# Attention and a gated MLP in one kernel: the last group takes x's seven combinations from DRAM, h's sums move to VectorE, partial sums are added by transfers

## The chip, the cores and the metric

One Trainium2 chip, one core. The metric is device microseconds of one execution, the median of the runs. All matrices are float32; the q, k, v, weight inputs arrive as float64 words and are converted on the chip.

## The reference, cut to what matters

```python
# q, k, v: (8, 8, 576, 64); block-causal softmax attention per head, then
x = attn_out.transpose(0, 2, 1, 3).reshape(4608, 512)
gate = 1.0 / (1.0 + np.exp(-(x @ w_gate)))      # w_gate, w_val: (512, 1536)
val = x @ w_val
return (gate * val @ w_out).astype(np.float32)  # w_out: (1536, 512)
```

## The kernel before, in words

The 1536 hidden columns are worked in three groups of 512. **The first group** runs beside the attention, batch by batch, with ordinary products; its output (a partial sum of the result, 4608 x 512) goes to the DRAM tensor `part_d`, and the attention output goes, transposed, to `xT_d`. **The second group** (the first loop over `k` near the end, six blocks of 768 tokens) and **the last group** (the second loop, again six blocks) use a seven-product scheme: the 2 x 2 blocks of a matrix product are formed from seven products of sums of blocks instead of eight products. Here they are called the second stage and the last stage.

A float32 product is made of three matmuls on "high" and "low" parts (a rounded copy, and the difference to it), so one of the seven products is 6 matmuls of 128x384 (`product`). Both loops need the seven combinations of x as high and low parts, 14 tiles called `XO` (names `XH`, `XL` in the trace). Per block they are made in this way: `x_load` brings x's four quarters from `xT_d` into `XB`, `x_sums` makes three sums on POOL, and `x_split` (second stage, lines 1196 to 1210) or `x_split_slots` (last stage, lines 1177 to 1194) copies the high parts on ACT and subtracts the low parts on VectorE (line 1204 and line 1183). There is one set of `XO`, so a slot is rewritten only when the last of the four units (two column halves, gate and value) has read it.

A block runs four `unit`s (168 matmuls), whose products are evicted by VectorE additions, a tanh on ACT and a multiplication on VectorE (line 1541) that gives h. In the second stage `out_block` then multiplies h by a plain `w_out` (72 matmuls of 128x512); `result` reads the old partial sum from `part_d`, adds on POOL (line 1584) and writes to a second tensor `part2_d`. In the last stage the output product is a seven-product scheme too (`out_terms`, 84 matmuls), so h needs its own sums: `own_halves` and `second_sum` form them on POOL (lines 1433, 1439, 1443, 1447), and split them into five slots `S` (ACT lines 1420, 1424, 1456; VectorE lines 1421, 1425, 1451, 1457). The accumulators `C` of out_terms must be read by an addition at line 1486 before product 3 adds to them (line 1400 is every matmul of `product`). Results are transposed on VectorE (line 1492), added to the partial sum (line 1494; POOL, in the last block VectorE) and stored.

Between the two loops the weights of the last group, converted piece by piece in the second stage (`streamed`, through a staging tile `st` to `wgv_d`), are loaded back: four tiles `w` of 1792 KB as each unit of the last second-stage block ends (line 1679), and two tiles `wo` (line 1689).

The order on each engine is made by a scheduler at build time from data dependencies; `behind(a, b)` adds an order between two instructions of one engine. SP issues nearly all transfers, in order, and waits in that order.

Of the kernel before, what the change touches and what calls it, by code (L numbers as in the profile page):

```python
# [74 lines left out]
def attn_glu_kernel(ctx: ExitStack, tc: tile.TileContext, q, k, v, w_gate, w_val, w_out, out):  # L75
# [162 lines left out]
    with ExitStack() as s2:  # L238
# [819 lines left out]
        part2_d = dram.tile([NTOK, DM], F32, name="part2_d")  # L1058
# [63 lines left out]
        def fetch_o(g, d, j, held=False):  # L1122
            raw, T = cv_tiles()
            rawv = raw.rearrange("p (kh mh c n) w -> p kh mh c (n w)", kh=2, mh=2, c=4)
            r = (F1 + 4 * g + 2 * j) * P
            cols = w_out.rearrange("r (mh c e n) -> r mh e c n", mh=2, c=4, e=2)[:, :, d]
# [49 lines left out]

        def x_split_slots(XBs):

            def split(a, b, src):
                for j, XB in enumerate(XBs):  # L1180
                    x = XB[:, src:src + b - a]
                    nc.scalar.copy(out=XO[j][0][:, a:b], in_=x)
                    low = nc.vector.tensor_sub(out=XO[j][1][:, a:b], in0=x, in1=XO[j][0][:, a:b].bitcast(F32))  # L1183
                    if a in (3, 6) or (a == 1 and j):
                        for fh in range(2):
                            behind(low.ins, last2[f"B22{fh}"])

            split(0, 1, 0)
            for XB in XBs:
                nc.gpsimd.tensor_sub(out=XB[:, 0], in0=XB[:, 2], in1=XB[:, 5])  # L1190
            split(4, 6, 4)
            split(1, 3, 1)
            split(3, 4, 3)
            split(6, 7, 0)
# [196 lines left out]
        XO = [[x2.tile([P, 7, N2], F32R, name=f"X{e}{j}") for e in "HL"] for j in range(KC)]  # L1391
# [22 lines left out]
        def own_halves(q, i, h):  # L1414

            SL, B11, B12, B22, sums = terms
            fh, second = divmod(i, 2)

            def split(slot, x, low):
                nc.scalar.copy(out=slot[:, 0], in_=x)  # L1420
                low.tensor_sub(out=slot[:, 1], in0=x, in1=slot[:, 0].bitcast(F32))

            def part(slot, x, low):
                nc.scalar.copy(out=slot[:, 0, fh], in_=x)
                ins = low.tensor_sub(out=slot[:, 1, fh], in0=x, in1=slot[:, 0, fh].bitcast(F32))  # L1425
                if slot is SL[2]:
                    mark2(f"B22{fh}", ins)

            if q == 0:
                if second:  # L1430
                    return
                T1 = sums[fh]
                nc.gpsimd.tensor_sub(out=T1, in0=B12[:, fh], in1=B11[:, fh])
                part(SL[0], h, nc.gpsimd)
                part(SL[1], T1, nc.gpsimd)
                return
            if second:
                part(SL[2], h, nc.vector)
                nc.gpsimd.tensor_sub(out=B12[:, fh], in0=h, in1=B12[:, fh])
                B22.append(h)  # L1440
                if fh:
                    split(SL[4], B12[:, :2], nc.vector)
                    nc.gpsimd.tensor_add(out=B11[:, :2], in0=B11[:, :2], in1=B12[:, :2])
                return
            part(SL[3], h, nc.vector)
            old = B22[fh]
            nc.gpsimd.tensor_sub(out=old, in0=h, in1=B11[:, fh])
            if fh:
                for n, x in enumerate(B22):
                    nc.scalar.copy(out=SL[0][:, 0, n], in_=x)  # L1450
                    nc.vector.tensor_sub(out=SL[0][:, 1, n], in0=x, in1=SL[0][:, 0, n].bitcast(F32))
                B22.clear()

        def second_sum():
            SL, B11, B12, B22, sums = terms
            nc.scalar.copy(out=SL[1][:, 0], in_=B11[:, :2])
            nc.vector.tensor_sub(out=SL[1][:, 1], in0=B11[:, :2], in1=SL[1][:, 0].bitcast(F32))

        def dm_rows(dst, k, m, n):
# [3 lines left out]
                     dst[r:r + N2, 256 * m + 64 * c:256 * m + 64 * c + 64].rearrange("(t p) x -> p t x", p=32))  # L1463
                    for c in range(4)]

        def place(x):
            return x.rearrange("p (t x) -> p t x", x=64)

        def partial(pr, k, m, n):
            for rows_, src in dm_rows(part2_d, k, m, n):  # L1470
                nc.sync.dma_start(out=place(pr)[rows_], in_=src)

        def out_terms(k, Wo, prs, spare, end):
# [4 lines left out]
            p1, c22 = {}, {}  # L1478
            for d in range(2):
                product(1, A[d], Wo[d], True, SL[0])  # L1480
                p1[d] = hp3.tile([P, N2], F32, name="p1o") if d else m2.tile([P, N2], F32, name="p1", bufs=2)
                nc.scalar.copy(out=p1[d], in_=A[d])
            for d in range(2):
                product(5, C[d], Wo[d], True, SL[1])
                c22[d] = spare[d]["22"]()
                nc.vector.tensor_add(out=c22[d], in0=C[d], in1=p1[d])  # L1486
# [3 lines left out]
            def result(m, n, d, c, src=None):  # L1490
                pr = prs[m, n]
                nc.vector.transpose(out=c, in_=c if src is None else src)
                x = place(pr).rearrange("p t (e j) -> p t e j", e=2)[:, :, d]
                (nc.vector if end else nc.gpsimd).tensor_add(out=x, in0=x, in1=c.rearrange("p (t j) -> p t j", j=32))
                if d:
                    for i, (rows_, dst) in enumerate(dm_rows(out, k, m, n)):
                        (nc.scalar if end and i % 2 else nc.sync).dma_start(out=dst, in_=place(pr)[rows_])
# [259 lines left out]
```

## Time and profile before

| | us |
|---|---|
| median of 3 runs (1148.11 to 1155.28) | 1150.37 |
| the profiled execution's own time | 1148.83 |
| its span, first to last instruction | 1147.0 |
| attention with the first group | 0 to about 542 |
| second stage, six blocks | about 542 to 822 |
| last stage, six blocks | about 822 to 1147 |

A block of the second stage lasts 45.7 us, one of the last stage 51.3 to 51.9 us. "PE" is the matmul engine (TensorE), "DVE" VectorE, "ACT" ScalarE, "POOL" GpSimd, "SP" the engine that issues most transfers. A waiting time stands in square brackets in front of the instruction that waited, with what ended it. The granted clock of TensorE has two levels here, 1.00 (2.4 GHz) and 0.50 (1.2 GHz).

### The profile page before, as it was taken

Reading aid. Unit: us, or ns where it says so; the run is one execution under the profiler, and the core shown is the slowest. Engines: PE = TensorE matmul, PEld = TensorE weight load, DVE = VectorE, ACT = ScalarE, POOL = GpSimd, SP = SyncE. Lnnn points to the kernel's source line nnn. Section 1 sums busy time; section 2 is a strip of 40 time slices with the busy share of each in tenths; the row PEclk is TensorE's granted clock in tenths of the full one; section 3 lists DMA queues with packets and bytes.
Section 4 is the critical chain, followed back from the end, with each engine's and each line's share of the span. In section 5 each row is a group of like instructions: output and inputs, shape, how many; then the busy total and the mean of one; then the engine's idle time right before and its main releaser. Section 6 shows DMA issues by size and latency. Waiting matters only on the chain.

```text
span 1147.0 us, 20057 instructions
## 1 busy us (share of the span) xinstructions
PE 1091.6 (95%) x6653; PEld 949.7 (83%) x6653; DVE 959.0 (84%) x1617; ACT 623.4 (54%) x1377; POOL 643.1 (56%) x761
## 2 busy tenths in 40 slices
PE   8999999999999999999999999999888988989895
PEld 6677777877887788788999989999778988989795
DVE  6899989998888898596998897888958778786957
ACT  6888777777777777433535444345332515242321
POOL 3745598989898887101143624625545656647432
PEclk9999999999999999999999999999988989989898
DMA  8797578888888777433324733629964351524152
GB/s 165 169 183 162 152 175 210 178 205 172 208 174 207 169 187 180 150 107 91 113 93 161 267 128 139 224 98 353 318 218 116 73 133 33 138 83 84 28 111 55
DMA packets 341227, 178.02 MB, mean 155 GB/s; under 512 B 287412, under 2 KB 308260, under 8 KB 340356
## 3 DMA queue, kind: packets, MB, share of 16 engines
q1 hardware_dynamic: 321284, 151.42, 50.9%
q0 software_dynamic: 6272, 17.26, 5.9%
q10 hardware_dynamic: 13568, 8.06, 2.6%
q8 instruction: 53, 0.87, 0.3%
q14 instruction: 50, 0.41, 0.1%
HBM read 106.30 MB, written 49.18 MB: 136 GB/s over the span
## 4 chain that ended last, share of the span: by engine, by line
PE 72%; DVE 15%; DMA 4%; issue 2%; POOL 2%; ACT 2%; SPq 1%; DVEq 0%; ACTq 0%; POOLq 0%
PE b L1400 31%; PE bank L368 13%; PE m L180 11%; PE m L191 7%; PE m L1572 5%; DVE XL L1183 3%; PE b L1572 2%; PE bank L180 1%; SPq L302 1%; DVE S L1425 1%; PE m L1400 1%; DVE v L1541 1%; DMA rb<-r_d 1%; DMA wgv_d<-st 1%; DVE XL L1204 1%
## 5 line engine op out<-in xcount | busy, mean ns | idle before, releaser
L1400 PE MATMUL b<-XH,w 128*128 128x384 f32 x1344 | 349.6, 336 | 7.5 <-DVE b L1548 5.4
L1400 PEld LDWEIGHTS b<-XH,w 128*128 128x128 f32 x1344 | 245.0, 189 | 10.8 <-DVE b L1548 5.8
L1400 PE MATMUL b<-XL,w 128*128 128x384 f32 x672 | 225.4, 336 | 0.0
L1400 PEld LDWEIGHTS b<-XL,w 128*128 128x128 f32 x672 | 126.9, 189 | 0.8
L1584 POOL TENSOR_TENSOR pr<-pr,pr 128x512 f32<-128x512 f32 x36 | 57.0, 1591 | 111.1 <-ACT pr L1583 87.6
L1400 PE MATMUL b<-S,wo 128*128 128x384 f32 x360 | 84.6, 389 | 23.1 <-DVE pr L1486 18.4
L1400 PEld LDWEIGHTS b<-S,wo 128*128 128x128 f32 x360 | 74.8, 224 | 30.3 <-DVE pr L1486 20.3
L368 PE MATMUL bank<-G,VS 128*64 128x64 f32 (+3 forms) x1264 | 95.4, 305 | 1.0 <-POOL G L626 0.6
L368 PEld LDWEIGHTS bank<-G,VS 128*64 128x64 f32 x1264 | 64.8, 137 | 33.7 <-issue 7.4
L191 PE MATMUL m<-wo,hH 128*128 128x512 f32 x256 | 84.1, 395 | 0.0
L180 PE MATMUL m<-XH,wg 128*128 128x512 f32 x240 | 81.2, 395 | 1.2 <-ACT t L213 1.2
L180 PE MATMUL m<-XH,wv 128*128 128x512 f32 x240 | 80.8, 394 | 0.0
L497 DVE TENSOR_REDUCE nm<-bank 128x2 f32<-128x1024 f32 (+1 forms) x96 | 76.9, 801 | 2.1 <-ACT XB L509 0.5
L1527 ACT COPY p<-b 128x384 f32<-128x384 f32 x48 | 22.8, 475 | 86.9 <-PE b L1400 84.3
L1537 ACT ACTIVATE g<-g 128x384 f32<-128x384 f32 x72 | 37.6, 525 | 57.4 <-DVE g L1561 28.9
L1572 PE MATMUL m<-wo,hH 128*128 128x512 f32 x192 | 63.5, 397 | 0.0
L191 PEld LDWEIGHTS m<-wo,hH 128*128 128x128 f32 x256 | 47.8, 188 | 10.7 <-ACT ost L986 0.9
L180 PEld LDWEIGHTS m<-XH,wg 128*128 128x128 f32 x240 | 45.1, 188 | 10.7 <-ACT t L213 1.7
L180 PEld LDWEIGHTS m<-XH,wv 128*128 128x128 f32 x240 | 45.0, 188 | 9.6 <-DVE h L217 0.2
L509 ACT ACTIVATE Z<-bank,nm 128x512 f32<-128x512 f32 (+3 forms) x96 | 49.3, 530 | 6.0 <-DVE nm L497 2.5
L191 PE MATMUL m<-wo,hL 128*128 128x512 f32 x128 | 51.3, 401 | 0.0
L509 ACT ACTIVATE XB<-bank,nm 128x512 f32<-128x512 f32 (+3 forms) x96 | 49.3, 530 | 3.5 <-DVE nm L497 1.9
(273 smaller groups left out, 2939.3 us busy)
## 6 DMA issues: line engine op xcount, KB each, us to landing
wgv_d<-st SPq DMA_DIRECT2D x12, 896.0 KB
XB<-xT_d SPq DMA_DIRECT2D x16, 576.0 KB
pr<-part_d SPq DMA_DIRECT2D x36, 256.0 KB
part_d<-pr SPq DMA_DIRECT2D x36, 256.0 KB
rqk<-in_q_dram SPq DMA_DIRECT2D x120, 72.0 KB
rqk<-in_k_dram SPq DMA_DIRECT2D x120, 72.0 KB
w<-wgv_d SPq DMA_DIRECT2D x4, 1792.0 KB
xT_d<-xT SPq DMA_DIRECT2D x24, 288.0 KB
```

Source lines behind the costliest of these rows:

```text
L180: mm = nc.tensor.matmul(ps, lhsT=lh, rhs=rh, start=(i == 0), stop=(i == n - 1))
L191: mm = nc.tensor.matmul(ps, lhsT=lh[:, f, t * P:(t + 1) * P], rhs=rh, start=(f == i == 0), stop=(f == F1 - 1 and i == 2))
L302: ins = queue.dma_start(**kw)
L368: pe_last[:] = [pin("PE", nc.tensor.matmul(*args, **kw)).ins]
L497: mark("DVE", nc.vector.tensor_reduce(out=nm_()[:, c0:c0 + 2], in_=ps[:, :, c:c + n], axis=AX.X, op=ALU.max, negate=True))
L509: mark("ACT", nc.scalar.activation(out=dst, in_=src, func=AF.Exp, bias=nm_()[:, c0 + h:c0 + h + 1], accum_out=sm[:, 5 * h + i:5 * h + i + 1]))
L1183: low = nc.vector.tensor_sub(out=XO[j][1][:, a:b], in0=x, in1=XO[j][0][:, a:b].bitcast(F32))
L1400: mm = nc.tensor.matmul(ps, lhsT=lh, rhs=rh, start=(first and k == 0), stop=(k == n - 1), skip_group_check=not first)
L1527: nc.scalar.copy(out=p1, in_=A)
L1537: mark2("ACT", nc.scalar.activation(out=t, in_=c, func=AF.Tanh, scale=0.5))
L1572: mm = nc.tensor.matmul(po[t], lhsT=lh[:, f, t * P:(t + 1) * P], rhs=wo[:, f, e], start=(half == i == 0), stop=(half == 1 and i == len(tod ...
L1584: nc.gpsimd.tensor_add(out=ost, in0=ost, in1=old)
```

## The change

- The second stage stores the split combinations of each block to a new DRAM tensor `x_d` right after it made them (`x_keep`, seven transfers of 768 KB). The last stage loads them (`x_fetch`, seven transfers in the order in which the products use the slots) instead of loading x and making sums and splits. `x_split_slots` is gone.
- The sums of h are made on VectorE, after the pieces that are due earlier, with `behind` holding them there; POOL keeps only two of them per block (T1 of the first column half).
- The second stage's `result` no longer loads the old partial sum, adds and stores: a transfer issued by POOL adds the block to `part_d` in DRAM. `part2_d` is gone; the last stage loads `part_d` and stores the result in pieces of 128 columns instead of 64.
- The staging tile `st` has two buffers instead of one, and the last conversion of a weight piece comes one place earlier.

```diff
-        part2_d = dram.tile([NTOK, DM], F32, name="part2_d")
+        x_d = dram.tile([NK, P, 7, 2 * KC, N2], F32, name="x_d")
...
+        X_ORDER = (0, 5, 4, 2, 1, 3, 6)
+        def x_keep(k):
+            for i in X_ORDER:
+                nc.sync.dma_start(out=x_d[k, :, i], in_=XOt[:, :, i].bitcast(F32))
+        def x_fetch(k):
+            for i in X_ORDER:
+                nc.sync.dma_start(out=XOt[:, :, i].bitcast(F32), in_=x_d[k, :, i])
...
+        def second_sums(c22):
+            SL, T1, T3 = terms
+            low = halves(SL[1], T1, nc.vector)
+            behind(low.ins, c22)
+            for fh, h in enumerate(seconds):
+                t = nc.vector.tensor_sub(out=T3[:, fh], in0=h, in1=T3[:, fh])
+                behind(t.ins, low.ins)
+            halves(SL[4], T3, nc.vector)
+            seconds.clear()
+        def last_sums(other):
+            SL, T1, T3 = terms
+            for fh, h in enumerate(firsts):
+                t = nc.vector.tensor_sub(out=T1[:, fh], in0=h, in1=T1[:, fh])
+                behind(t.ins, other)
+            halves(SL[0], T1, nc.vector)
+            firsts.clear()
...
-                ost = io.tile([P, DM], F32, name="pr0", bufs=4)
-                old = io.tile([P, DM], F32, name="pr1", bufs=2)
-                nc.sync.dma_start(out=old, in_=part_d[r:r + P, :])
+                ost = io.tile([P, DM], F32, name="pr0", bufs=3)
                 nc.scalar.mul(out=ost, in_=po[t], mul=0.5)
-                nc.gpsimd.tensor_add(out=ost, in0=ost, in1=old)
-                nc.sync.dma_start(out=part2_d[r:r + P, :], in_=ost)
+                nc.gpsimd.dma_start(out=part_d[r:r + P, :], in_=ost, accum_op=ALU.add)
...
-                st = io.tile([P, 2, 7, P], F32R, name="st")
+                st = io.tile([P, 2, 7, P], F32R, name="st", bufs=2)
...
-            if i == 2 or (i == 1 and k) or (i == 0 and k == NK - 1):
+            if (i == 2 and k < NK - 1) or (i == 1 and k) or (i == 0 and k >= NK - 2):
...
-            x_split(XBs, sums)
+            if k < NK - 1:
+                x_split(XBs, sums)
+                x_keep(k + 1)
+            else:
+                x_fetch(0)
...
             if not end:
-                x_split_slots(XBs)
-            for m, n in ((0, 0), (1, 0)):
-                partial(prs[m, n], k, m, n)
+                x_fetch(k + 1)
             run(block)
```

On VectorE, in the last stage's fourth block, from the multiplications that give h to the split of a sum (`XL`: low parts of x; `S`: low parts of h; L1486 the readings of the accumulators), before:

```order
L1541 SCALAR_TENSOR_TENSOR v_10669<-g_10609,v_10669 128x384
L1425 TENSOR_TENSOR S_9087<-t_10646,S_9087 128x384
L1541 SCALAR_TENSOR_TENSOR v_10667<-g_10607,v_10667 128x384
L1425 TENSOR_TENSOR S_9086<-v_10669,S_9086 128x384
L1486 TENSOR_TENSOR g_10745<-b,p_10729 128x384
L1425 TENSOR_TENSOR S_9086<-v_10667,S_9086 128x384
L1183 TENSOR_TENSOR XL_5851<-XB,XH_5850 128x768
L1183 TENSOR_TENSOR XL_5849<-XB,XH_5848 128x384
L1183 TENSOR_TENSOR XL_5851<-XB,XH_5850 128x384
L1486 TENSOR_TENSOR pr_9092<-b,p1o 128x384
L1561 TENSOR_TENSOR v_10668<-b,p_10651 128x384
L1421 TENSOR_TENSOR S_9088<-b_9090,S_9088 128x768
```

The same place in the changed kernel (L1424 and L1441 are h's sums into `XB`, L1473 the readings of the accumulators, L1432 the split of a sum):

```order
L1413 TENSOR_TENSOR S_9001<-t_10412,S_9001 128x384
L1530 SCALAR_TENSOR_TENSOR v_10435<-g_10375,v_10435 128x384
L1544 TENSOR_TENSOR v_10433<-b,v_10433 128x384
L1424 TENSOR_TENSOR XB<-v_10435,XB 128x384
L1530 SCALAR_TENSOR_TENSOR v_10433<-g_10373,v_10433 128x384
L1413 TENSOR_TENSOR S_9000<-v_10435,S_9000 128x384
L1424 TENSOR_TENSOR XB<-v_10433,XB 128x384
L1413 TENSOR_TENSOR S_9000<-v_10433,S_9000 128x384
L1473 TENSOR_TENSOR g_10506<-b,p_10491 128x384
L1473 TENSOR_TENSOR sp_9003<-b,p1o 128x384
L1432 TENSOR_TENSOR S_8999<-XB,S_8999 128x768
L1441 TENSOR_TENSOR XB<-v_10433,XB 128x384
```

The three low parts of x between the two readings of the accumulators are gone; the two readings stand next to each other, with two sums of h ahead of them and four behind.

On SP, where the second stage ends, before (`w` and `wo`: weights of the last stage, `st`: converted pieces, XB<-xT_d: x for the next block):

```order
L1679 DMA w_8689<-wgv_d 128x3584
L1638 DMA wgv_d<-st 128x1792
L1679 DMA w_8779<-wgv_d 128x3584
L1585 DMA part_d<-pr_8581 128x512
L1582 DMA pr_8982<-part_d 128x512
L1091 DMA raw<-in_moe_w_out_dram 128x4x64 x4
L1679 DMA w_8841<-wgv_d 128x3584
L1638 DMA wgv_d<-st 128x1792
L1679 DMA w_8941<-wgv_d 128x3584
L1585 DMA part_d<-pr_8975 128x512
L1582 DMA pr_8988<-part_d 128x512
L1164 DMA XB<-xT_d 128x2x384
```

The same place in the changed kernel (XO<-x_d: the slots of x for the last stage's first block):

```order
L1666 DMA w_8649<-wgv_d 128x3584
L1666 DMA w_8739<-wgv_d 128x3584
L1382 DMA XO<-x_d 128x4x384 x4
L1625 DMA wgv_d<-st 128x1792
L1666 DMA w_8801<-wgv_d 128x3584
L1382 DMA XO<-x_d 128x4x384 x2
L1666 DMA w_8901<-wgv_d 128x3584
L1382 DMA XO<-x_d 128x4x384
L1625 DMA wgv_d<-st 128x1792
L1680 DMA wo_8994<-wgv_d 128x3584
L1680 DMA wo_8995<-wgv_d 128x3584
L1382 DMA XO<-x_d 128x4x384 x7
```

The seven slots stand between the weights of the last stage, in one queue with them, and behind a store of a converted piece.

## Rows read from the trace of the kernel before

**Rows 1.** The page, the span in 40 slices: the clock granted to PE, in tenths

```profile
PEclk9999999999999999999999999999988989989898
```

**Rows 2.** Busy by stretch: stretch, length, PE, PEld, DVE, ACT, POOL, clock, DMA share, GB/s

```profile
695.74:741.48 45.74, 45.74 (x242) 42.75 (x241) 37.77 (x63) 19.78 (x36) 19.54 (x16) 1.00 0.47 153
768.00:815.00 47.00, 44.01 (x220) 40.07 (x219) 42.16 (x72) 20.94 (x36) 20.52 (x17) 0.96 1.01 349
815.00:850.00 35.00, 28.38 (x139) 26.50 (x138) 21.65 (x34) 9.24 (x18) 19.18 (x14) 0.90 0.90 300
887.00:938.30 51.30, 47.06 (x254) 45.92 (x253) 40.03 (x64) 18.80 (x36) 29.74 (x28) 0.93 0.41 94
```

**Rows 3.** PE in order of time, the output product of the last stage's second block

```profile
910.99 2.24 PE L1400 MATMUL m<-S,wo 128*128 128x384 f32 x12
...
916.19 1.62 PE L1400 MATMUL b<-S,wo 128*128 128x384 f32 x6
921.38 2.61 PE L1400 MATMUL b<-S,wo 128*128 128x384 f32 x7 [3.57 <-DVE pr L1486]
924.51 5.66 PE L1400 MATMUL b<-S,wo 128*128 128x384 f32 x23 [0.53 <-DVE S L1457]
...
934.18 0.33 PE L1400 MATMUL b<-XH,w 128*128 128x384 f32 x1
```

**Rows 4.** DVE in order of time, the same place, and one row of the last block

```profile
908.54 0.95 DVE L1183 TENSOR_TENSOR XL<-XB,XH 128x768 fp32r<-128x768 f32 x1
...
916.54 4.32 DVE L1183 TENSOR_TENSOR XL<-XB,XH 128x768 fp32r<-128x768 f32 x3
920.78 0.55 DVE L1486 TENSOR_TENSOR pr<-b,p1o 128x384 f32<-128x384 f32 x1
921.71 0.94 DVE L1421 TENSOR_TENSOR S<-b,S 128x768 fp32r<-128x768 f32 x1
...
1122.82 2.03 DVE L1421 TENSOR_TENSOR S<-b,S 128x768 fp32r<-128x768 f32 x1
```

**Rows 5.** PE in order of time, the output product of the last block

```profile
1118.41 2.24 PE L1400 MATMUL m<-S,wo 128*128 128x384 f32 x12
...
1134.03 2.25 PE L1400 MATMUL b<-S,wo 128*128 128x384 f32 x12
```

**Rows 6.** POOL in order of time, beside rows 4

```profile
916.27 2.03 POOL L1443 TENSOR_TENSOR b<-b,b 128x768 f32<-128x768 f32 x1
```

**Rows 7.** PE in order of time, from the second stage to the last

```profile
810.79 0.50 PE L1572 MATMUL m<-wo,hL 128*128 128x512 f32 x1 [2.39 <-DVE hL L1412]
...
822.05 0.33 PE L1400 MATMUL b<-XH,w 128*128 128x384 f32 x1
...
827.58 0.44 PE L1400 MATMUL b<-XH,w 128*128 128x384 f32 x1 [1.18 <-DVE g L1548]
...
840.60 0.69 PE L1400 MATMUL b<-XH,w 128*128 128x384 f32 x1 [5.45 <-DVE b L1548]
...
859.68 2.24 PE L1400 MATMUL m<-S,wo 128*128 128x384 f32 x12
```

**Rows 8.** The chain that ended last, the same place

```profile
828.30 9.50 DMA wgv_d<-st
```

**Rows 9.** SP's loads of x in that block, and stretches of 2 us as in rows 2

```profile
923.15 1.92 SPq L1164 DMA_DIRECT2D XB<-xT_d  x4
...
888.00:890.00 2.00, 2.00 (x13) 2.00 (x12) 1.11 (x2) 0.58 (x2) 0.00 (x0) 1.00 1.01 185
...
925.00:927.00 2.00, 2.00 (x8) 2.00 (x8) 1.89 (x3) 0.98 (x2) 1.25 (x1) 0.50 0.99 368
927.00:929.00 2.00, 2.00 (x12) 2.00 (x11) 1.03 (x3) 0.00 (x0) 0.00 (x0) 0.86 1.01 370
```

**Rows 10.** POOL's transfers into part_d at the end of the first group

```profile
L998 POOL DMA_DIRECT2D part_d<-ost x4: 532/533/553, 541.4 to 543.0; - x4
...
DMA to landing us min/median/max: 2.3/5.7/6.4
```

More of the change, by code (lines that the diff above doesn't have):

```diff
@@ L1175, in x_sums @@
             return eng.tensor_sub(out=XB[:, 5], in0=XB[:, 3], in1=XB[:, 4]).ins
[L1177 to L1194, printed above, removed]
         def x_split(XBs, other=None):
@@ L1390, in attn_glu_kernel @@
         W = {(0, 0): wgv_tile(0, 0)}
-        XO = [[x2.tile([P, 7, N2], F32R, name=f"X{e}{j}") for e in "HL"] for j in range(KC)]
+        XOt = x2.tile([P, 2 * KC, 7, N2], F32R, name="XO")
+        XO = [[XOt[:, 2 * j + e] for e in range(2)] for j in range(KC)]
+        X_ORDER = (0, 5, 4, 2, 1, 3, 6)
[5 more added lines that the diff above has]
+                nc.sync.dma_start(out=XOt[:, :, i].bitcast(F32), in_=x_d[k, :, i])
         def product(i, ps, w, first, term=None):
@@ L1414, in own_halves @@
         def own_halves(q, i, h):
-            SL, B11, B12, B22, sums = terms
+            SL, T1, T3 = terms
             fh, second = divmod(i, 2)
[L1419 to L1427, printed above, removed]
@@ L1429, in own_halves, with part @@
-            if q == 0:
[L1430 to L1435, printed above, removed]
+            def part(slot, low):
+                nc.scalar.copy(out=slot[:, 0, fh], in_=h)
+                low.tensor_sub(out=slot[:, 1, fh], in0=h, in1=slot[:, 0, fh].bitcast(F32))
+            if q == 0:
+                if not second:
+                    part(SL[0], nc.gpsimd)
+                    nc.gpsimd.tensor_sub(out=T1[:, fh], in0=T3[:, fh], in1=h)
+                    if fh:
+                        halves(SL[1], T1, nc.gpsimd)
@@ L1448, in own_halves @@
[L1448 to L1459, printed above, removed]
+                part(SL[2], nc.vector)
@@ new lines, in own_halves, with halves @@
+                nc.vector.tensor_sub(out=T1[:, fh], in0=h, in1=T1[:, fh])
+                seconds.append(h)
+                return
+            part(SL[3], nc.vector)
+            firsts.append(h)
+        def halves(slot, x, low):
+            nc.scalar.copy(out=slot[:, 0], in_=x)
+            return low.tensor_sub(out=slot[:, 1], in0=x, in1=slot[:, 0].bitcast(F32))
+        seconds, firsts = [], []
+        def second_sums(c22):
[7 more added lines that the diff above has]
+            seconds.clear()
@@ L1464, in dm_rows @@
[L1464 to L1471, printed above, removed]
+                     dst[r:r + N2, 128 * c:128 * c + 128].rearrange("(t p) x -> p t x", p=32)) for c in range(4)]
         def out_terms(k, Wo, prs, spare, end):
```

70 lines of the change are left out of this document (31 added, 39 removed).

## The prediction

> **What bounds the kernel now.** I read the clock on the page first. PE's granted clock is full up to the 28th of the 40 slices and then dips in most of them [rows 1]: something interrupts PE in the last stage only. The stretches say how much. A block of the second stage keeps PE busy for all of its 45.74 us at clock 1.00; a block of the last stage lasts 51.30 us, with 47.06 us busy at a mean clock of 0.93 [rows 2]. So nothing that only relieves ACT, POOL or VectorE in the second stage can gain, and the second stage can only lose. In the last stage PE waits.
>
> PE's order of time shows where. From 910.99 to 916.19 thirty matmuls go out, 0.173 us each. The next six are followed by a wait of 3.57 us for VectorE's line 1486, and after it 23 matmuls take 5.66 us, 0.24 us each [rows 3]: the granted clock is 0.50 in that stretch and back at 0.86 in the next [rows 9]. VectorE's row ahead of line 1486 is the three low parts of x, 4.32 us together [rows 4]. They contain one operation of 128x768 and two of 128x384; a 128x768 alone took 0.95 us. POOL ran its 128x768 sum of h in the same time [rows 6]. So VectorE's order decides: work that is due a block later stands ahead of a reading for which PE waits, and the wait is paid a second time in clock.
>
> The other lost stretch is the change of stage. PE waits 2.39 us, 1.18 us and 5.45 us there [rows 7]; the last goes back to a store of a converted piece that had to leave the single staging tile, 9.50 us [rows 8]. The transfer engines are at 1.01 and 0.90 of their time in these 82 us [rows 2].
>
> **Removed in the last stage: x's sums and splits.** The output product is 84 matmuls, 14.6 us at 0.173. From its first matmul to the next block's first matmul the second block takes 934.18 - 910.99 = 23.2 us [rows 3]. The last block splits no x any more, and its output product takes 1134.03 + 2.25 - 1118.41 = 17.9 us [rows 5], with one product of a hidden unit (1.04 us) among it as in the others: 15.6 us would be free of waits. Blocks one to five should thus come to about 17.9 us, if nothing else changed. The hidden part of a block is already dense: 51.3 - 23.2 = 28.1 us for 162 matmuls, again 0.173.
>
> **Moved: h's sums to VectorE.** VectorE gets six operations of 128x384 in the tail (two each for T1, T3 and the last sum). The rows of this size start 0.47 us apart (920.78 to 921.71 holds two of them [rows 4]), so 2.8 us. In return the ones it has are no longer stretched: the same split of a sum took 0.94 us without, and 2.03 us in the last block with POOL beside it [rows 4]; and ACT need not wait for POOL's 2.03 us sum before it copies the high part [rows 6]. Walking the new order with 0.47 and 0.87 us per operation, both readings of the accumulators are done 4.8 us after the output product starts, where product 3 wants them at 5.2 us; the split for product 7 is done at 9.0 us, wanted at 9.4 us; the last split, for product 4, at 14.5 us, wanted at 13.7 us. One wait of 0.8 us and some tenths: 17.2 us, between 15.6 us (all hidden) and 17.9 us (the last block as it is). Five blocks gain 5 x (23.2 - 17.2) = 30 us, bounds 26.5 and 38. The last block gains 0.7 us by the same chain, and its stores are half as many with twice the columns; I take 1.5 us together, bounds 0 and 3.
>
> **Added in the last stage: seven loads per block.** They are 5.5 MB in pieces of 1536 bytes. The nearest row: four loads of x, 1.57 MB in similar pieces, went through in 4 us at 368 and 370 GB/s [rows 9], so 15 us. A slot may be loaded once the last unit has read it. The first is free 6 us before the output product starts, the last 5 us after; they are wanted from 17 to 24 us after. At 370 GB/s the last lands at about 11 us, so PE, with its 17.2 us, hides them all; the cost is 0. In the other bound they go at the 185 GB/s of the pieces of 256 bytes [rows 9], take 30 us and end at 24 us: still about hidden. The Trainium skill has a rule against this ("DMA: Bandwidth & Descriptors", Anatomy of one DMA): every transfer costs about 2 us besides its bytes, so seven in a row of 768 KB each would need some 27 us, and the change of stage, by an estimate from this rule, 12 us more, about 1127 us. Here four loads together took 4 us, so these fixed parts overlapped; the trace speaks against reading the rule as a sum.
>
> **The change of stage.** What goes: the low parts of x for the next block, the wait for the staging tile (two buffers, and one conversion earlier), so the three waits on VectorE. Their cost: from 822.05 to 859.68 are 37.6 us for work of 28.1 us [rows 7], 9.5 us; and 2.39 us in a stretch of 47 us with a mean clock of 0.96 [rows 2], which is 3.8 us at half speed or 1.9 us lost: 13.8 us in all. What comes: the new order on SP puts the seven slots between the four weight tiles, in one queue. From 768 us on the engines are full at 349 GB/s [rows 2]. The first slot is free when the last unit has done its first product: the output product of 45.7 - 168 x 0.173 = 16.6 us and seven more products of 1.04 us lie between that and 822 us, so at about 798 us. Four slots take 9 us and, with what is queued, land by 812 us; then come a piece (0.9 MB), a weight tile (1.8 MB), two slots, a tile and the last slot, 6.9 MB or 20 us: 832 us, and up to 9 us later if the six adding transfers of the last block (3 MB at twice their bytes) take their turn among them. The first unit wants the last slot 7.3 us after its start, at 829 us. I leave 8 us of the 13.8 for that wait and its clock: a gain of 6 us, bounds a gain of 12 and a loss of 10.
>
> **Added in the second stage.** Stores of x, 5.5 MB per block, 15 us of the transfer engines. A block has them busy for 0.47 x 45.74 = 21.5 us [rows 2]; the six loads of old partial sums (1.57 MB, 4 us) go, the adding transfers come in place of the plain stores. No row shows an adding one. The nearest are POOL's plain ones: 0.53 us of POOL's time each, landing after 2.3 to 6.4 us [rows 10]; at twice the traffic, 4 us more per block. Together 33 to 37 us of 45.74 us: there is room. POOL itself issues six for 3.2 us instead of adding; the x for its sums waits behind the stores in the queue, 15 + 4 us, the six sums take 6 us more by half of the 2.03 us in [rows 6], and the split wants them 29 us (168 matmuls) after the block's start. The first conversion after the first store comes close to the addition queued behind it on VectorE, for which PE's accumulators wait: I take a loss of 2 us, bounds 0 and 8. ACT is behind an adding transfer only if three buffers are all in flight; the groups of three are 36 matmuls or 8.3 us apart, above 6.4.
>
> **Sum.** -30 - 1.5 - 6 + 2 = -35.5 us, from the profiled execution's 1148.83 us: 1113.3 us. It was 1.5 us below the median of the runs shown, so the median of the changed kernel should be about 1115 us; its own range is 1104 to 1126.
>
> **Rivals.**
> - *VectorE's chain decides the tail.* Each sum waits for a high part from ACT, and ACT's copies stand behind those of the accumulators. If every split comes 2 us later than walked, a block's tail is 19.5 us, and five blocks gain 18.5 us: 1126 us. For it: VectorE is the engine that every wait in the tail names. Against it: the last block manages 17.9 us with POOL in the way.
> - *The change of stage takes the gain.* The queue is full for 80 us already, and the kept and fetched slots add 11 MB to it, 30 us at 370 GB/s, against some 10 MB that go later or are gone. If the first unit's slots come 20 us late, 1115 + 14 = 1129 us; with the tail of the first rival 1140 us. For it: the share of 1.01. Against: half of the removed traffic is in the same stretch.
> - *Slower: the stores of x fill the transfer engines in the second stage.* At 185 GB/s they take 30 us; with the other 21.5 us less 4 and up to 4 more they come to 51 us per block of 45.74 us. Then the next split waits for the store that reads its slot, 6 us in each of five blocks, and the change of stage is 2 x 15 us later: 1115 + 30 + 30 = 1175 us. It decides from about 24 us for the stores, 230 GB/s. For it: nobody stored in pieces of 1536 bytes so far. Against: converted pieces were stored in the stretch at 349 GB/s.
> - *The waits only change their name:* each block's loads of x are held up by the results' stores ahead of them in SP's order, and PE waits 6 us for a slot instead of for VectorE: 1115 + 5 x 6 = 1145 us. Against: in the new order a hidden part, 28 us, lies between those stores and the next loads.
>
> **How the numbers follow.** Forecast 0.57, first rival 0.17, second 0.13, slower 0.08, the same wait 0.05. A measurement of this kernel can tell about 1% from no change, 11.5 us. Faster by over 1% takes the forecast, the first rival and most of the second: 0.86. Within 1%: the end of the second and the last: 0.06. Slower by over 1%: 0.08. The range leaves 2 in 10 out: from 1103 us, the best bounds of tail and change of stage nearly together, to 1134 us, which holds the first rival and the better part of the second.
>
> **What would show it.** Right: in the last stage no wait of PE above 1 us within a block, the clock at 1.00 in all but the first, blocks of 45 to 46 us, POOL idle in the first 14 us of the output product, PE's waits at the change of stage named by transfers into `XO`. Wrong: PE waiting for `XO` in every block (loads too slow), for the splits of sums by over 2 us (VectorE's chain), or any second-stage block longer than 46.5 us (stores of x or adding transfers).

## The result and the profile after

The changed kernel takes 1115.59 us (median of 4 runs, 1114.55 to 1118.36) against 1151.21 us before (4 runs, one more than in the table ahead, 1148.11 to 1155.28): a ratio of 0.9692 (95% interval 0.9656 to 0.9729). The forecast was 1115 us. The profiled execution took 1118.36 us, the highest of the four, with a span of 1116.6 us, so the two profiles are only 30.5 us apart. They divide as follows; the borders are the first matmuls of output products, as PE's order of time has them. The third row is the change of stage.

| stretch | before, us | after, us | difference | forecast |
|---|---|---|---|---|
| start to the second stage's first output product | 569.3 | 566.7 | -2.6 | 0 |
| to the second stage's last output product | 231.0 | 239.7 | +8.7 | +2 |
| to the last stage's first output product | 59.4 | 56.0 | -3.4 | -6 |
| five blocks of the last stage | 258.7 | 224.4 | -34.3 | -30 |
| last output product to the end | 28.6 | 29.8 | +1.2 | -1.5 |
| span | 1147.0 | 1116.6 | -30.4 | -35.5 |

So the total came out nearly as forecast, but two rows of the table did not: the first, and the second stage. The first row is scatter: in the fourteen kernels profiled for this study that border lies between 564.6 and 569.3 us, and a kernel with the same instructions as before up to there (the first experiment) has it at 565.5.

The granted clock on the page, to be held against [rows 1]; the dips of the last stage are gone but for one slice:

```profile
PEclk9999999999999999999999999999899999999998
```

By stretch, with the columns of [rows 2]: a block of the second stage, two stretches of the change of stage, and the second block of the last stage.

```profile
695.74:741.48 45.74, 45.74 (x241) 42.75 (x241) 34.70 (x61) 21.04 (x36) 17.05 (x18) 1.00 0.83 252
...
778.00:825.00 47.00, 41.16 (x204) 37.90 (x203) 25.98 (x51) 13.84 (x26) 8.94 (x9) 0.93 1.06 334
825.00:862.40 37.40, 30.56 (x158) 29.69 (x157) 12.94 (x24) 9.03 (x18) 6.57 (x7) 0.91 0.88 303
...
907.73:952.50 44.77, 44.20 (x254) 43.59 (x254) 31.46 (x60) 13.23 (x24) 14.35 (x13) 1.00 0.68 195
```

A block of the last stage went from 51.30 to 44.77 us with the clock at 1.00, although its transfer engines went from 0.41 to 0.68. A second-stage block went from 0.47 to 0.83 of the transfer engines and kept its 45.74 us. At the change of stage the clock is still down (0.93 and 0.91).

PE in order of time over that block's output product, which answers to [rows 3]:

```profile
907.73 2.24 PE L1392 MATMUL m<-S,wo 128*128 128x384 f32 x12
909.81 2.24 PE L1392 MATMUL b<-S,wo 128*128 128x384 f32 x12
911.89 1.20 PE L1392 MATMUL b<-XO,w 128*128 128x384 f32 x6
912.93 4.33 PE L1392 MATMUL b<-S,wo 128*128 128x384 f32 x24
917.44 2.32 PE L1392 MATMUL b<-S,wo 128*128 128x384 f32 x12 [0.18 <-DVE g L1491]
919.60 2.24 PE L1392 MATMUL m<-S,wo 128*128 128x384 f32 x12
921.68 0.34 PE L1392 MATMUL b<-S,wo 128*128 128x384 f32 x1
922.40 2.18 PE L1392 MATMUL b<-S,wo 128*128 128x384 f32 x11 [0.38 <-DVE S L1432]
924.42 1.89 PE L1392 MATMUL b<-XO,w 128*128 128x384 f32 x10
```

The wait of 3.57 us is gone. The tail (from the output product's first matmul to the next block's first) is 924.42 - 907.73 = 16.7 us instead of 23.2, and two waits of 0.18 and 0.38 us are left. VectorE beside it, as in [rows 4] (L1473 reads the accumulators, L1432 splits a sum):

```profile
911.41 0.55 DVE L1473 TENSOR_TENSOR g<-b,p 128x384 f32<-128x384 f32 x1
912.09 0.56 DVE L1473 TENSOR_TENSOR sp<-b,p1o 128x384 f32<-128x384 f32 x1
913.00 0.96 DVE L1432 TENSOR_TENSOR S<-XB,S 128x768 fp32r<-128x768 f32 x1 [0.35 <-ACT S L1431]
...
915.87 0.95 DVE L1432 TENSOR_TENSOR S<-XB,S 128x768 fp32r<-128x768 f32 x1
...
921.43 0.92 DVE L1432 TENSOR_TENSOR S<-XB,S 128x768 fp32r<-128x768 f32 x1
```

And the seven loads of x beside the same product, in stretches with the columns of [rows 2] (the last two columns, share of the transfer engines and GB/s, are the ones to read):

```profile
904.00:908.00 4.00, 4.00 (x25) 4.00 (x24) 2.62 (x6) 0.51 (x1) 0.00 (x0) 1.00 1.01 341
908.00:910.00 2.00, 2.00 (x14) 2.00 (x13) 2.00 (x5) 0.99 (x2) 0.00 (x0) 1.00 1.06 389
...
916.00:918.00 2.00, 1.82 (x11) 1.53 (x10) 2.00 (x4) 0.50 (x1) 0.00 (x0) 1.00 1.06 368
918.00:920.00 2.00, 2.00 (x14) 2.00 (x13) 2.00 (x5) 0.81 (x1) 0.00 (x0) 1.00 0.30 106
919.00:920.00 1.00, 1.00 (x8) 1.00 (x7) 1.00 (x3) 0.81 (x1) 0.00 (x0) 1.00 0.07 25
```

Nearly all of them runs from 904 to about 918.6 us (0.2 MB comes before, a last 25 KB by 920 us), some 4 to 6 us ahead of the next block's first product. Now the change of stage in PE's order of time, which answers to [rows 7]:

```profile
794.89 11.65 PE L1392 MATMUL b<-XO,w 128*128 128x384 f32 x55 [5.84 <-ACT p L1516]
...
831.55 1.28 PE L1392 MATMUL b<-XO,w 128*128 128x384 f32 x6 [3.28 <-DMA XO<-x_d]
833.63 3.62 PE L1392 MATMUL b<-XO,w 128*128 128x384 f32 x12 [0.80 <-DMA XO<-x_d]
840.01 22.54 PE L1392 MATMUL b<-XO,w 128*128 128x384 f32 x120 [2.76 <-DMA XO<-x_d]
862.39 2.24 PE L1392 MATMUL m<-S,wo 128*128 128x384 f32 x12
```

The three waits on VectorE of [rows 7] are gone. In their place stand three for slots of x, 6.84 us, and ahead of them, still in the second stage, one of 5.84 us that names a copy on ACT. ACT's order tells why that copy is late:

```profile
793.80 0.67 ACT L1079 ACTIVATE cT<-raw 128x512 f32<-128x512 f32 x1 [10.44 <-DMA raw<-in_moe_w_out_dram]
794.38 0.46 ACT L1516 COPY p<-b 128x384 f32<-128x384 f32 x1
```

It stands behind the first step of a weight conversion, which waits 10.44 us for its raw piece. The piece is late on SP:

```profile
757.24 8.36 SPq L1378 DMA_DIRECT2D x_d<-XO  x6
765.83 7.43 SPq L1698 DMA_DIRECT2D XB<-part_d  x5
773.35 2.34 SPq L1378 DMA_DIRECT2D x_d<-XO  x1
775.73 4.07 SPq L1698 DMA_DIRECT2D XB<-part_d  x3
779.90 12.43 SPq L1091 DMA_DIRECT2D raw<-in_moe_w_out_dram  x7
```

Seven stores of x and eight loads of partial sums, which the last stage wants only about 100 us later, stand ahead of it. Last, at the end of the kernel, VectorE has no gap from 1094.88 us to its last addition, POOL does nothing, and PE has been done since 1101.48 + 2.18 = 1103.66 us:

```profile
1094.88:1109.33 14.45, 8.22 (x45) 7.29 (x43) 14.45 (x30) 1.35 (x2) 0.00 (x0) 0.89 0.13 24
```

### The profile page after: what moved, and what is told of

Its sections match the earlier page's. It is cut to its first block, busy times and chain, and to the rows that moved or that the text cites. A ratio compares the mean times of both kernels' runs of the same rounds, so it can differ in the third digit from the quotient of the medians.

```text
span 1116.6 us, 19735 instructions
## 1 busy us (share of the span) xinstructions
PE 1076.9 (96%) x6653; PEld 938.0 (84%) x6653; DVE 890.0 (80%) x1589; ACT 591.0 (53%) x1309; POOL 525.0 (47%) x679
## 4 chain that ended last, share of the span: by engine, by line
PE 67%; DVE 17%; DMA 7%; issue 2%; SPq 2%; POOL 2%; ACT 2%; ACTq 0%; DVEq 0%; POOLq 0%
PE b L1392 26%; PE bank L368 12%; PE m L180 11%; PE m L191 7%; PE m L1561 4%; PE b L1561 2%; DMA XO<-x_d 2%; PE bank L180 1%; DVE S L1432 1%; SPq L302 1%; PE m L1392 1%; DMA rqk<-in_q_dram 1%; DVE v L1530 1%; DMA rqk<-in_k_dram 1%; DVE XO L1185 1%
## 5 line engine op out<-in xcount | busy, mean ns | idle before, releaser
L1392 PE MATMUL b<-XO,w 128*128 128x384 f32 x2016 | 363.2, 338 | 13.9 <-DMA XO<-x_d 6.8
L1392 PEld LDWEIGHTS b<-XO,w 128*128 128x128 f32 x2016 | 355.3, 190 | 18.6 <-ACT p L1516 7.1
L1571 POOL DMA_DIRECT2D part_d<-pr x36 | 32.7, 972 | 133.0 <-ACT pr L1570 132.6
L1392 PE MATMUL b<-S,wo 128*128 128x384 f32 x360 | 68.8, 338 | 3.6 <-DVE S L1432 2.3
L1392 PEld LDWEIGHTS b<-S,wo 128*128 128x128 f32 x360 | 62.1, 188 | 7.6 <-DVE S L1432 4.2
L1481 POOL TENSOR_TENSOR XB<-XB,g 128x384 f32<-128x384 f32 x15 | 18.3, 1220 | 89.2 <-DVE g L1479 89.2
L191 PE MATMUL m<-wo,hL 128*128 128x512 f32 x128 | 51.3, 401 | 0.0
L180 PE MATMUL m<-XL,wv 128*128 128x512 f32 x120 | 47.5, 396 | 0.0
```

The lines of the kernel that those rows point to most:

```text
L180: mm = nc.tensor.matmul(ps, lhsT=lh, rhs=rh, start=(i == 0), stop=(i == n - 1))
L191: mm = nc.tensor.matmul(ps, lhsT=lh[:, f, t * P:(t + 1) * P], rhs=rh, start=(f == i == 0), stop=(f == F1 - 1 and i == 2))
L1392: mm = nc.tensor.matmul(ps, lhsT=lh, rhs=rh, start=(first and k == 0), stop=(k == n - 1), skip_group_check=not first)
L1571: nc.gpsimd.dma_start(out=part_d[r:r + P, :], in_=ost, accum_op=ALU.add)
```

## Experiments

Each median is of the kernel's own runs; the ratio is to the kernel before on the same chip. Where two changed kernels were not run together, differences of their medians are rough; they are then compared by these ratios or by their traces.

**1. The order alone, in the kernel before.** Three low parts of x go behind the second accumulator reading.

```diff
-                        for fh in range(2):
-                            behind(low.ins, last2[f"B22{fh}"])
+                        behind(low.ins, last2["C22"])
```

> The kernel before, with one order changed: the three low parts of x that stood ahead of the second accumulator reading on VectorE stand behind it. Theory (the wait of 3.57 us came from that order, but the 4.32 us of x's low parts still have to be done by VectorE in the output product): the wait of 3.57 us goes, later splits of h's sums or the next block's first products wait instead, the tail of a block goes from 23.2 us to about 20.5 us, five blocks gain some 13 us: 1138 us (1130 to 1145). Rival 1 (the order alone was the fault, taking x's sums away was not needed): a tail of 17 to 18 us, 1120 to 1126 us. Rival 2 (the wait only changes its name): 1147 to 1152 us.

1147.11 us, ratio 0.9976 (0.9954 to 0.9999). PE and then VectorE in order of time, second block:

```profile
920.36 6.04 PE L1399 MATMUL b<-S,wo 128*128 128x384 f32 x23 [4.39 <-DVE S L1456]
```

```profile
913.29 3.87 DVE L1183 TENSOR_TENSOR XL<-XB,XH 128x768 fp32r<-128x768 f32 x3
```

The wait for the reading is gone, and a longer one (4.39 us) for the split of a sum, behind the same low parts of x, has taken its place. Blocks two to five last 51.2 us each, where those of the kernel before last 51.3 to 52.6; the five blocks together take 256.4 us instead of 258.7, half a microsecond less per block. Theory and first rival fall, the second rival holds: in this order at least the wait changes its name. Orders that put the low parts behind the splits as well were not tried.

**2. h's sums back on POOL, x still loaded.**

```diff
-                t = nc.vector.tensor_sub(out=T3[:, fh], in0=h, in1=T3[:, fh])
-                behind(t.ins, low.ins)
+                nc.gpsimd.tensor_sub(out=T3[:, fh], in0=h, in1=T3[:, fh])
```

(and the other four sums in the same way)

> The changed kernel with the six sums of h per block back on POOL and no held order for them; x's combinations are still loaded. Theory (x's low parts ahead of the readings made most of the tail; h's sums on VectorE bring the smaller part, through POOL no longer stretching VectorE's operations): each tail about 17.9 us, as in the last block of the kernel before, instead of 16.7 us: six times 1.2 us, about 1122 us (1118 to 1128). Rival 1 (moving h's sums made the gain): tails above 21 us, 1137 us or more. Rival 2 (the move of h's sums is worth nothing): 1114 to 1117 us.

1118.7 us, ratio 0.9733 (0.971 to 0.9755); the interval overlaps the changed kernel's. The second block, from output product to output product:

```profile
905.11 2.24 PE L1392 MATMUL m<-S,wo 128*128 128x384 f32 x12
...
950.00 1.20 PE L1392 MATMUL m<-S,wo 128*128 128x384 f32 x6
```

Blocks two to five last 44.89 us, where the changed kernel's last 44.77: with x's sums gone, h's sums cost a tenth of a microsecond per block on POOL, not 1.2. So the time lies in the theory's range, but not for the theory's reason. The first rival falls. The tail's gain belongs to x.

**3 and 4. Plain partial sums.** Loads of the old sum, additions on POOL and plain stores, first in the place of the changed kernel's three buffers (two and one), then with the buffers of before (four and two), for which the second staging tile had to go.

```diff
-                nc.gpsimd.dma_start(out=part_d[r:r + P, :], in_=ost, accum_op=ALU.add)
+                nc.sync.dma_start(out=old, in_=part_d[r:r + P, :])
...
+                nc.gpsimd.tensor_add(out=ost, in0=ost, in1=old)
+                nc.gpsimd.dma_start(out=part_d[r:r + P, :], in_=ost)
```

> The changed kernel with the second stage's partial sums made as before: load of the old sum by SP, addition on POOL, plain store (issued by POOL). Theory (the second stage's loss comes from x's stores and from what queues behind them on SP, not from the adding transfers): within 3 us of the changed kernel, 1113 to 1120 us. Rival (the adding transfers, 8.7 us from issue to landing, hold up the stage): faster by 5 us or more, below 1111 us. Other rival (the loads of the old sums are in the way of the full queue at the change of stage): slower by 5 us or more, above 1121 us.

> As the kernel with plain partial sums (1163 us), but with the buffers that the kernel before gives them (four and two) and therefore one staging tile. Theory now (the loads of the old sums stand on SP behind x's transfers in a full queue, and ACT waits for a free result buffer, so h's copies behind it are late): the buffers move the wait but do not remove it, at least 15 us above the kernel with one staging tile alone. Rival (my cut to two and one buffers made the loss): within 5 us of the kernel with one staging tile alone.

1163.39 us (ratio 1.0116, 1.0088 to 1.0144) and 1126.35 us (0.9784, 0.9756 to 0.9812). With two and one buffers ACT stands still in front of h's copies until a buffer of the second stage's results is stored, and that result waits for a load that stands behind six loads of x on SP:

```profile
899.14 0.93 ACT L1412 CAST S<-XB 128x384 fp32r<-128x384 f32 x2 [19.30 <-DMA part_d<-pr]
```

PE waits 25.1 us for that copy. The sign is that of the other rival, the loads in the way of the full queue, but with the old buffers 37 of the 48 us are gone again, so it was mostly my cut of the buffers, and the second expectation's theory falls as well (7.3 us above one staging tile alone, not 15; nor within 5, as its rival has it).

**5. One staging tile in the changed kernel.**

```diff
-                st = io.tile([P, 2, 7, P], F32R, name="st", bufs=2)
+                st = io.tile([P, 2, 7, P], F32R, name="st")
```

> The changed kernel with one staging tile instead of two for the converted weight pieces. Theory (the single staging tile cost the kernel before 5.45 us of waits and clock after it at the change of stage, and would cost it again with more in the queue): 7 to 14 us slower, 1122 to 1130 us. Rival (with the conversion one place earlier and no low parts of x in that stretch, the second tile brings nothing): 1113 to 1118 us.

1119.06 us, ratio 0.9725 (0.9701 to 0.9749): 3.5 us, half of the least that the theory asked, and the interval overlaps the changed kernel's. Waits of 2.04 and 3.79 us for VectorE appear in the second stage. The second of them comes where the changed kernel waits 5.84 us for ACT, a wait that this kernel does not have; its second stage is 3.1 us longer, its change of stage 1.2 us shorter.

**6. Of the change, x's transfers nearly alone:** the edits of 2, of 4 with the old buffers, and of 5 together. What stays of the rest is the wider pieces of the partial sums, their plain stores issued by POOL, the conversion one place earlier and the new arrangement of h's sums.

> Of the change only the stored and loaded combinations of x (with the partial sums' wider pieces): plain partial sums with the buffers of before, one staging tile, h's sums on POOL. Theory (x's sums alone make the tail, but the queue at the change of stage cannot carry them without the other edits): tails of 17 us in the last stage, five blocks gain 30 us, the change of stage loses 25 us or more: 1135 to 1160 us. Rival (the other edits are not needed): 1113 to 1122 us.

1127.98 us, ratio 0.9807 (0.9784 to 0.9831). Better than the theory allowed: blocks two to five last 44.87 us, the first 51.4. So x's transfers, with these smaller edits, give 22 of the 35.6 us. From here the changed kernel is reached by h's sums (1126.35 us, 1.6 us less, with ratios whose intervals overlap), the adding transfers (1119.06) and the second staging tile (1115.59, again with overlapping intervals).

**7. The eight loads of partial sums behind the last stage's weights on SP.**

```diff
+                    if k == 0:
+                        behind(part.ins, wo_load.ins)
```

> The changed kernel with one order on SP: the eight loads of partial sums for the last stage's first block (1.5 MB, 11.5 us of SP's time in the changed kernel) stand behind the last stage's weights instead of among x's stores of the second stage's last block. Theory (PE's 5.84 us wait in that block is the full queue: the weight piece that ACT and VectorE convert stands on SP behind six stores of x and these loads): the wait gets shorter by about 4 us, the slots come up to 4 us earlier, 4 to 9 us gained, 1107 to 1112 us. Rival (the piece is late for a reason of its own, the order on SP is not it): 1113 to 1118 us.

1112.81 us, ratio 0.9671 (0.9648 to 0.9693), between the ranges of theory and rival, and by the interval not to be told from the changed kernel. The trace decides. The wait of 5.84 us is gone entirely:

```profile
779.67 16.97 PE L1392 MATMUL b<-XO,w 128*128 128x384 f32 x97
796.48 0.39 PE L1561 MATMUL m<-wo,hH 128*128 128x512 f32 x1
```

The last stage's first output product starts at 850.66 us instead of 862.39, of which 1.0 us is the scatter of the first stretch. But its first block lasts 50.61 us instead of 45.34:

```profile
854.89 0.44 PE L1392 MATMUL b<-S,wo 128*128 128x384 f32 x1 [1.99 <-ACT S L1431]
856.77 3.89 PE L1392 MATMUL b<-S,wo 128*128 128x384 f32 x11 [1.44 <-POOL S L1432]
```

The order that the build made for ACT there differs: the copy of a sum (L1431) stands behind two copies of accumulators (L1469), in the changed kernel ahead of them. Half of the gain is given back by a place that the edit never touched. The kernel of experiment 4 has the same two waits and a first block of 50.36 us, against 44.76 us with one staging tile, so most of the 7.3 us between these two lies in that block. There too the copy of the sum stands behind a copy of an accumulator; that the order, and not the plain sums themselves, costs these 5.6 us is argued from the trace and was not tested.

**8. The last stage starts with the block that the slots still hold.** Its seven stores and seven loads are left out; the other five blocks follow.

```diff
-                x_keep(k + 1)
-            else:
-                x_fetch(0)
+                if k < NK - 2:
+                    x_keep(k + 1)
...
-        for k in range(NK):
-            end = k == NK - 1
+        blocks = [NK - 1, *range(NK - 1)]
+        for k in blocks:
+            end = k == blocks[-1]
...
-                x_fetch(k + 1)
+                x_fetch(blocks[blocks.index(k) + 1])
```

> The changed kernel with the last stage's blocks in another order: it starts with the block whose combinations the slots of x still hold, so seven stores and seven loads of 768 KB, 11 MB or 30 us of the transfer engines, are gone at the change of stage. Theory (the full queue costs the changed kernel some 18 us there: waits of 5.84 us for a late weight piece, 3.28, 0.80 and 2.76 us for slots of x, and the clock after them): the three waits for slots go, the 5.84 us mostly go, 10 to 15 us gained: 1101 to 1106 us. Rival 1 (the late weight piece has nothing to do with x's stores): 5.84 us and its clock stay, 1107 to 1110 us. Rival 2 (the four weight tiles then are the late ones): under 4 us gained, above 1112 us.

1096.87 us (1096.48 to 1098.74), ratio 0.9545 (0.9527 to 0.9562): 18.7 us below the changed kernel by the medians, 17 us by the ratios, and better than the theory. By stretch, from the place where the wait of 5.84 us was to the last stage's first output product:

```profile
780.30:826.00 45.70, 45.70 (x243) 42.78 (x242) 28.75 (x55) 15.57 (x30) 9.44 (x10) 1.00 0.94 302
826.00:841.00 15.00, 15.00 (x88) 15.00 (x88) 8.07 (x16) 5.09 (x10) 5.78 (x5) 1.00 1.07 309
```

PE has no gap and the clock stays at 1.00. That output product starts at 841.07 us, 21.3 us earlier, of which 2.0 us are the scatter of the first stretch. So the changed kernel lost some 19 us here, 12.7 us in the waits and, by an estimate from its mean clock (47.0 us at 0.93 and 37.4 us at 0.91), 6.7 in the clock.

**9 and 10. Two edits again where the queue has room:** the kernel of 8 with the edits of 4 and 5, and with those of 2.

> The kernel whose last stage starts with the block that the slots still hold (1096.9 us), but with plain partial sums in the buffers of before and one staging tile; with the first block loaded, these two edits made 1126.4 us of 1115.6 us. Theory (they count only because the queue is full at the change of stage; 11 MB less leave room): within 4 us of 1096.9 us. Rival (they cost the same whatever the queue holds): 1105 to 1110 us.

> The kernel whose last stage starts with the block that the slots still hold (1096.9 us), but with h's sums on POOL. Theory (with x's low parts gone it hardly matters which engine makes h's sums: tails of 44.88 us blocks instead of 44.77 us): 1097 to 1099 us. Rival (the 3 us measured for this edit in the changed kernel belong to the sums): 1099.5 to 1102 us.

1106.88 us (1102.56 to 1110.11; ratio 0.9643, 0.9589 to 0.9697) and 1100.02 us (0.9581, 0.9548 to 0.9614). The theory of the first falls: 10 us remain, as its rival said. But the places are others than in experiment 4, where 5.6 us lay in the last stage's first block. In the trace, 7.6 us longer, 3.0 us lie before the second stage's first output product, in the scatter, and 4.6 us in the second stage, with a wait of 2.65 us for VectorE, whose conversion of a weight piece stands ahead of the addition that PE needs; so what the two edits cost here is 5 to 10 us. Of the second's 3 us the trace shows only 0.1 us per block, 0.3 us in the second stage and 0.4 us at the end; 1.9 us lie before the second stage's first output product. The interval overlaps that of experiment 8, and whether h's sums are worth 1 us or 3 stays open.

**11. x's combinations stored twice.**

```diff
                 x_keep(k + 1)
+                x_keep(k + 1)
```

> The changed kernel storing x's seven combinations twice per block of the second stage: 5.5 MB or 15 us of the transfer engines more in each block. Theory (the transfer engines were at 0.82 of a 45.7 us block, so with 0.33 more they are the bound): second-stage blocks of 50 to 54 us, and the backlog delays the change of stage: 1140 to 1170 us. Rival (x's stores lie in time that nothing else wants, so a second set is hidden too, at least before the change of stage): 1116 to 1130 us.

1162.87 us, ratio 1.0128 (1.0084 to 1.0172). The time is the theory's, the place is not: the second stage lasts 243.2 us to its last output product, where the changed kernel's lasts 239.7, and almost everything is paid in one wait at the change of stage.

```profile
PE b L1392 <- DMA XO<-x_d: 43.6, 2, 40.0
```

(waits of PE: us in total, times, longest). Here seven more transfers per block hardly stop PE in the second stage; the delay shows where PE next needs the slots of x through the same queue.

**12. x's combinations loaded twice.**

```diff
                 x_fetch(k + 1)
+                x_fetch(k + 1)
```

> The changed kernel loading x's seven combinations twice per block of the last stage. In the changed kernel the seven loads go through from 904.0 to 918.6 us, 370 GB/s, and the next block's first product starts at 924.4 us: 5.8 us of cover for the first slot, some 13 us for the last. Theory (cost of one set 0, of a second set what exceeds the cover): the last slot lands at about 933 us against 931.7 us, 1 to 4 us per block with the clock, 1121 to 1136 us. Rival (the loads are already at the edge, every added us counts): 14 us per block, 1175 us or more. Other rival (a second set is hidden as well): 1114 to 1119 us.

1138.54 us, ratio 0.9917 (0.9891 to 0.9944). Five blocks last 48.1 to 50.9 us, some 5 us more each, for 15 us of additional transfers; two or three waits for slots per block, 2.6 to 3.3 us together, and the clock behind them:

```profile
908.48:958.77 50.29, 46.45 (x253) 44.82 (x253) 31.45 (x60) 13.24 (x24) 14.27 (x13) 0.97 0.94 285
```

So one set is hidden, with about 10 us to spare (an estimate: 15 us of transfers more for 5 us): the theory's mechanism, 2.5 us dearer than its range.

## Why the prediction was right, and where its terms were off

**The tail, the main term, was right in its parts.** Forecast 17.2 us, measured 16.7. The walk along VectorE holds nearly to the tenth: the readings were to be done 4.8 us after the product's start and are (912.09 + 0.56 - 907.73 = 4.9); the split for product 7 was put at 9.0 (915.87 + 0.95 - 907.73 = 9.1), the last one at 14.5 (921.43 + 0.92 - 907.73 = 14.6). The remaining wait was put at 0.8 us and is 0.56. Five blocks gave 34.3 us instead of 30: 0.5 us per block from the tail, 2.2 because I took the second block's 51.30 us for all, while the third to fifth lasted 51.6 to 52.6 (the section on the profile before gives 51.9 as the longest), less 0.6 us for the changed kernel's first block of 45.34.

**Its reason was too narrow.** I wrote that VectorE's order decides. Experiment 1 shows that another order of the same work brings half a microsecond per block, of some 7, and experiment 2 that moving h's sums, with the order held for them, brings a tenth. What counts is that x's sums and splits are out of the tail. VectorE's low parts stand ahead of what PE waits for in both orders, 3.57 us before and 4.39 us in experiment 1; ACT's copies and POOL's sums of x went with them, and no run separates the three. That POOL's sums of h stretch VectorE's operations, the other reason given for the move, was worth no more than that tenth.

**The loads in the last stage cost nothing, as forecast.** The last was to land 11 us after the product's start; nearly all is in at 10.9 and the last packets by 12.3, and experiment 12 measures the cover. The Trainium skill ("DMA: Bandwidth & Descriptors", Anatomy of one DMA) gives a transfer issued by GpSimd a fixed part of about 2.0 us, most of it completion latency. Adding it up for seven transfers issued by SP, as the prediction did, is an estimate of 27 us beyond what that section states; the trace has 14.6 us for nearly all of the bytes and some 18 us from the first issue to the last packet, so the measurement decides against the sum here.

**The change of stage came out near its value, the second stage did not.** 8 us were left for the slots and their clock; PE waited 6.84 us, and the clock behind these waits took some 3.4 us more by the estimate of experiment 8. The last slot kept PE until 840.0 us, within the 832 to 841 of the forecast. The step that failed is "I take a loss of 2 us" in the second stage, at 8.7 us above its bound of 8; 7.1 of these lie in its last interval from output product to output product, 53.7 us instead of 46.7. With it one of the prediction's own signs of being wrong came true, a second-stage block longer than 46.5 us. The place was nearly named (a conversion with an addition queued behind it), but I looked at VectorE after x's first store, where no wait is longer than 0.7 us, and not at what stands ahead of the raw pieces on SP in the last two blocks. The eight early loads of partial sums I did not count at all: a transfer wanted in the next stage had been moved up into a queue that the change fills. Experiment 7 shows that they make the wait of 5.84 us, experiment 8 that without the transfers of x's first block (11 MB against 1.5 MB) neither this wait nor those for slots are left. Some of the second rival (the change of stage takes the gain) has thus come true: second stage and change of stage together are 5.3 us slower where 4 us faster was forecast, 9 of that rival's 14 us.

**The end.** 1.5 us of gain were forecast, 1.2 us of loss measured. PE is done 16.8 us after the product's start instead of 17.9, as the chain said. But VectorE then needs 5.7 us more instead of 4.2, and from its last addition to the end it takes 7.3 us instead of 6.5. With h's sums on POOL (experiment 2) VectorE needs 5.1 us, so h's sums are 0.6 of the 1.5 us, and yet that kernel's end is no shorter (30.2 us). Where the rest comes from, and whether the wider stores cost the 0.8 us after it, was not tested.

**The total.** Tail and scatter (-4.3, -2.6) and the second stage, change of stage and end (+6.7, +2.6, +2.7) leave the profile 5.1 us above the sum; and the profiled execution lies 2.8 us above its median, that of before 2.4 us below. So the median agrees to 0.6 us partly by luck.

**The slower rival** needed stores of x at under 230 GB/s. They did not get there: from 716 to 722 us, with the queue to themselves, they went at 363 GB/s. Experiment 11 shows the margin: twice the bytes, and the kernel is slower than before, though by the backlog at the change of stage far more than by longer blocks.

## What to carry to other kernels

Work that is repeated from the same inputs was worth storing and loading back here, because it stood in the chain that PE waited for and the transfer engines had room in that stage. Read the share stage by stage, and ask of each set of data whether it has to travel at all (the block still in place needed neither store nor load, 17 to 19 us). In a queue that is worked in order, read what stands ahead of each piece that an engine waits for, above all transfers for a later stage. And where a scheduler makes the order, compare it again after every edit: with one copy behind two others on ACT, a block took 5 us longer after an edit on SP.

## What was not expected of the hardware

- An adding transfer takes POOL longer to issue than a plain one, and it lands later. The 36 of the changed kernel, and the 36 plain ones of the same 256 KB in the kernel of experiment 4 with the old buffers (durations in ns, landing in us; minimum, median and maximum):

```profile
L1571 POOL DMA_DIRECT2D part_d<-pr x36: 857/869/1577, 599.4 to 844.7; - x36
...
DMA to landing us min/median/max: 4.1/8.7/11.9
```

```profile
L1574 POOL DMA_DIRECT2D part_d<-pr x36: 539/557/585, 603.1 to 856.2; - x36
...
DMA to landing us min/median/max: 2.3/5.9/8.8
```

  Without the transfers of x's first block it is the same: 7.5 us in the median for the adding ones (experiment 8), 5.4 us for the plain ones (the first kernel of experiments 9 and 10). The forecast had counted 0.53 us [rows 10] and assumed 8.3 us to be long enough for ACT never to wait; ACT waited 9.6 us for them in all, 8 times.
- Seven transfers of 768 KB in pieces of 1536 bytes went through in about 14.6 us but for their ends, at 341 to 389 GB/s in the stretches shown, with the transfer engines' share at 1.01 to 1.06 in them.
- 5.5 MB more per block of the second stage (experiment 11) lengthened the stage by 3.5 us only, up to its last output product; the delay appeared 40 us long at one wait behind it.
